# Loading the first token block as two column parts, one on each DMA queue, ahead of everything else, with the matmuls in alternating order

## The chip, the cores and the metric

The kernel runs on one core of a Trainium2 chip. The metric is the time of one execution on the device, in microseconds (us); lower is better. The profile's span, from the first to the last instruction, is about 1.5 us shorter than that time.

## The reference

Two matrix products with a SiLU between them, in bf16, for 2048 tokens of width 640 and a hidden width of 1728:

```python
B, S, D, F = 1, 2048, 640, 1728
def reference(x, w1, w2):
    h = jnp.einsum("bsd,df->bsf", x, w1)
    h = _silu(h)
    out = jnp.einsum("bsf,fd->bsd", h, w2)
    return out
```

## The kernel before

The matmuls of this kernel read tokens with their features on the partitions. For the first chunk of 512 tokens (four blocks of 128) TensorE makes that itself: it multiplies each 128x128 piece of x by an identity matrix (`transpose`), and ScalarE and VectorE copy the result from PSUM to `xT`. The other three chunks come through transposing DMAs later. The first 512 columns of w1 come in five slabs of 128 rows, one for each feature tile d. `early(d, j0, j1)` multiplies slab d with blocks j0 to j1-1, as soon as both are there. Before any data has landed TensorE runs matmuls on constants (`busy`), the warm-ups.

The issue order of the loads, on the two queues (SP and ACT):

```python
        def on_sync(sp):
            # load_x(j): block j, 160 KB.   load_slab(d): slab d, 128 KB
            load_x(0)
            for d in range(0, DT, 2):
                load_slab(d)
            for j in range(2, TPC):
                load_x(j)
            for g, (a, b) in enumerate(((FB, FM), (FM, F))):   # the rest of w1
                sp.dma_start(
                    out=w1_sb[:, :, a:b], in_=w1_v[:, :, a:b]
                ).then_inc(sem_w1g[g], 16)
            sp.wait_ge(sem_w1g[1], 16)
            # ... transposing loads of chunks 1 to 3, then w2 ...

        def on_scalar(act):
            act.dma_start(
                out=x_sb[:, 1, :], in_=xf[P:2 * P, :]
            ).then_inc(sem_xb[1], 16)
            for d in range(1, DT, 2):
                act.dma_start(
                    out=w1_sb[:, d, 0:FB], in_=w1_v[:, d, 0:FB]
                ).then_inc(sem_w1[d], 16)
            # ...
```

TensorE's early phase (W_FIRST = 12, W_SECOND = 15):

```python
            busy(W_FIRST)
            need(sem_id, 2)
            busy(W_SECOND)
            transpose(0)
            transpose(1)
            for j in range(2):
                for d in range(TA):          # TA = 2
                    early(d, j, j + 1)
            early(2, 0, 2)
            early(3, 0, 2)
            transpose(2)
            early(4, 0, 2)
            transpose(3)
            for d in range(3):
                early(d, 2, 3)
            for d in range(3):
                early(d, 3, 4)
            for d in range(3, DT):
                early(d, 2, 4)
            # ... from here on: 512-wide matmuls, 240 + 20 of the first product, 294 of the second
```

## Time and profile before

| | before |
|---|---|
| time, median of the first three executions | 127.17 us (126.99 to 127.23) |
| span of the profiled execution | 125.7 us |
| first transpose starts | 3.76 us |
| clock opens (first start after which 128-wide matmuls follow 56 ns apart instead of 107) | 6.3 us |
| first 512-wide matmul of the main phase starts | 10.47 us |

First, from the page of the kernel before: the span, the busy time of each engine, and the chain of work that ended last.

```profile
span 125.7 us, 1492 instructions
...
PE 123.1 (98%) x661; PEld 60.4 (48%) x661; DVE 12.2 (10%) x20; ACT 37.0 (29%) x65; POOL 0.7 (1%) x6
...
PE 98%; ACT 0%; issue 0%
PE ps L343 47%; PE ps L309 41%; PE ps L254 4%; PE ps L223 2%; PE ps L300 2%; PE ps L239 1%; ACT o_sb L380 0%
```

TensorE (PE) is the chain: nothing else holds up the end. Lines 343, 309 and 300 are the main phase; 223 are the warm-ups, 239 the transposes and 254 the early matmuls. The change touches only the last three, 7.8% of the span (2.4, 1.4 and 4.0%).

Next, the timeline of TensorE up to 11 us. The columns are start, busy us, engine and line, what it is, the count, and in brackets idle time before it with what ended that.

```profile
0.78 3.04 PE L223 MATMUL ps<-const-bfloat16-1.0 128*128 128x128 bf16 x27 [0.78 <-PEq L421]
3.76 1.25 PE L239 MATMUL ps<-ident,x_sb 128*128 128x128 bf16 x10
4.80 2.63 PE L254 MATMUL ps<-xT,w_sb 128*128 128x128 bf16 x24
7.26 0.44 PE L239 MATMUL ps<-ident,x_sb 128*128 128x128 bf16 x5
7.54 0.60 PE L254 MATMUL ps<-xT,w_sb 128*128 128x256 bf16 x4
7.98 0.44 PE L239 MATMUL ps<-ident,x_sb 128*128 128x128 bf16 x5
8.26 2.38 PE L254 MATMUL ps<-xT,w_sb 128*128 128x128 bf16 x32
10.47 0.81 PE L309 MATMUL ps<-xT,w_sb 128*128 128x512 bf16 x3
```

Matmuls overlap (a warm-up is listed with 312 ns and the next starts after 107), so the busy column is no measure of holes. Those show in the single starts of the trace: on the slow clock one 128-wide matmul starts every 107 ns, its slot, and what a step is longer than that is a hole. Below, "cold" is time before the clock opens and "warm" time after it, and a load "lands" when its completion is signalled. Before the first transpose the step is 256 ns, a hole of 0.15 us; there is no other in the early phase.

### The profile page before, as it was taken

What the parts mean: (1) busy time and instruction counts of PE and PEld (TensorE: products, weight loads), DVE (VectorE), ACT (ScalarE), POOL (GpSimd) and SP (SyncE); (2) the same over time, 40 slices, a digit from 0 to 9 for tenths busy, and PEclk for the clock granted to TensorE, in tenths of its full rate; (3) what the DMA queues carried; (4) which work ended last, traced back from release to release, by engine and by line L of the source; (5) the groups of instructions that cost most, each with busy time, mean ns of one, the idle gap of its engine ahead of it and who ended that gap; (6) DMA issues with size and microseconds to landing.
All of it is one profiled execution on the core that took longest, in us unless ns stands there. A gap on an engine that the chain in (4) does not pass through costs nothing.

```text
span 125.7 us, 1492 instructions
## 1 busy us (share of the span) xinstructions
PE 123.1 (98%) x661; PEld 60.4 (48%) x661; DVE 12.2 (10%) x20; ACT 37.0 (29%) x65; POOL 0.7 (1%) x6
## 2 busy tenths in 40 slices
PE   7999999999999999999999999999999999999994
PEld 7996444444444444444444444443444443444452
DVE  0330000000000000000000000000700003920421
ACT  3327655555555555555540000001500000000000
POOL 2000000000000000000000000000000000000000
DMA  3992999992000000000000000000346000631022
GB/s 106 350 374 89 216 201 201 273 387 83 0 0 0 0 3 0 0 0 5 0 0 0 0 0 0 0 5 0 73 94 219 0 0 0 257 113 52 0 104 94
DMA packets 17014, 10.37 MB, mean 82 GB/s; under 512 B 10736, under 2 KB 17008, under 8 KB 17008
## 3 DMA queue, kind: packets, MB, share of 16 engines
q1 hardware_dynamic: 16432, 9.82, 26.8%
q10 hardware_dynamic: 576, 0.46, 1.1%
q8 instruction: 5, 0.08, 0.3%
q14 instruction: 1, 0.01, 0.0%
HBM read 5.16 MB, written 2.62 MB: 62 GB/s over the span
## 4 chain that ended last, share of the span: by engine, by line
PE 98%; ACT 0%; issue 0%
PE ps L343 47%; PE ps L309 41%; PE ps L254 4%; PE ps L223 2%; PE ps L300 2%; PE ps L239 1%; ACT o_sb L380 0%
## 5 line engine op out<-in xcount | busy, mean ns | idle before, releaser
L309 PE MATMUL ps<-xT,w_sb 128*128 128x512 bf16 x240 | 52.0, 379 | 0.0
L343 PE MATMUL ps<-w_sb,hT 128*128 128x512 bf16 (+2 forms) x221 | 45.6, 367 | 0.0
L373 ACT ACTIVATE hT<-ps 128x512 bf16<-128x512 f32 x52 | 30.6, 598 | 23.9 <-PE ps L309 22.2
L309 PEld LDWEIGHTS ps<-xT,w_sb 128*128 128x128 bf16 x240 | 23.5, 98 | 28.1
L343 PEld LDWEIGHTS ps<-w_sb,hT 128*128 128x128 bf16 x221 | 20.8, 98 | 24.6 <-issue 0.6
L399 DVE CAST o_sb<-ps 128x512 bf16<-128x512 f32 (+1 forms) x16 | 10.0, 677 | 104.7 <-PE ps L343 104.7
L343 PE MATMUL ps<-hT,w_sb 128*128 128x512 bf16 x52 | 11.4, 379 | 0.0
L380 ACT CAST o_sb<-ps 128x128 bf16<-128x128 f32 x1 | 0.3, 266 | 34.2 <-PE ps L343 34.2
L380 ACT CAST oT<-ps 128x512 bf16<-128x512 f32 x4 | 2.1, 599 | 22.3 <-PE ps L343 22.3
L343 PEld LDWEIGHTS ps<-hT,w_sb 128*128 128x128 bf16 x52 | 5.0, 98 | 6.3 <-issue 0.4
L254 PE MATMUL ps<-xT,w_sb 128*128 128x128 bf16 (+1 forms) x60 | 5.6, 258 | 0.0
L254 PEld LDWEIGHTS ps<-xT,w_sb 128*128 128x128 bf16 x60 | 4.8, 111 | 0.2
L223 PE MATMUL ps<-const-bfloat16-1.0 128*128 128x128 bf16 x27 | 3.0, 312 | 0.8 <-PEq L421 0.8
L223 PEld LDWEIGHTS ps<-const-bfloat16-1.0 128*128 128x128 bf16 x27 | 2.8, 148 | 0.7 <-issue 0.7
L392 DVE CAST xT<-ps 128x384 bf16<-128x384 f32 x4 | 2.2, 558 | 6.8 <-PE ps L239 6.8
L366 ACT CAST xT<-ps 128x256 bf16<-128x256 f32 x4 | 1.5, 372 | 3.5 <-PE ps L239 3.5
L300 PE MATMUL ps<-xT,w_sb 128*64 128x512 bf16 x20 | 2.3, 381 | 0.0
L343 PE MATMUL ps<-w_sb,hTl 64*128 64x512 bf16 (+2 forms) x17 | 2.2, 366 | 0.0
L239 PE MATMUL ps<-ident,x_sb 128*128 128x128 bf16 x20 | 2.1, 265 | 0.0
L361 ACT ACT_TABLE_LOAD x1 | 1.3, 1283 | 2.1 <-issue 2.1
L239 PEld LDWEIGHTS ps<-ident,x_sb 128*128 128x128 bf16 x20 | 1.7, 120 | 0.2 <-DMA x_sb<-in_x_dram 0.2
L300 PEld LDWEIGHTS ps<-xT,w_sb 128*64 128x64 bf16 x20 | 1.0, 110 | 1.2 <-ACT hT L373 0.4
(11 smaller groups left out, 3.7 us busy)
## 6 DMA issues: line engine op xcount, KB each, us to landing
out_dram<-o_sb SPq DMA_DIRECT2D x15, 160.0 KB, 1.8
w_sb<-in_w_dram SPq DMA_DIRECT2D x1, 1120.0 KB, 7.6
w_sb<-in_w_dram SPq DMA_DIRECT2D x1, 960.0 KB, 5.6
w_sb<-in_w_dram SPq DMA_DIRECT2D x1, 880.0 KB, 7.2
w_sb<-in_w_dram SPq DMA_DIRECT2D x1, 640.0 KB, 5.2
x_sb<-in_x_dram SPq DMA_DIRECT2D x3, 160.0 KB, 4.0
w_sb<-in_w_dram SPq DMA_DIRECT2D x3, 128.0 KB, 3.4
w_sb<-in_w_dram ACTq DMA_DIRECT2D x2, 128.0 KB, 3.8
```

The source lines that it names most:

```text
L223: pe.matmul(ps[:, KF - 1, 0:P], lhsT=ones[:, 0:P], rhs=ones[:, 0:P], start=True, stop=True,)
L239: ins = pe.matmul(ps[:, ba + (d >= TA), k * P:(k + 1) * P], lhsT=x_sb[:, j, d * P:(d + 1) * P], rhs=ident[:, :], start=True, stop=True,)
L254: ins = pe.matmul(ps[:, f, j0 * P:j1 * P], lhsT=w1_sb[:, d, f * P:(f + 1) * P], rhs=xT[:, d, j0 * P:j1 * P], start=(d == 0 and j0 == 0), s ...
L300: ins = pe.matmul(ps[h * FL:(h + 1) * FL, b, :], lhsT=w1_sb[:, d, NF * P:F], rhs=xT[:, d, (c + h) * CH:(c + h + 1) * CH], start=(d == 0), ...
L309: ins = pe.matmul(ps[:, b, :], lhsT=w1_sb[:, d, f * P:(f + 1) * P], rhs=xT[:, d, c * CH:(c + 1) * CH], start=(d == 0), stop=(d == DT - 1),)
L343: ins = pe.matmul(ps[:, bank, 0:width], lhsT=w_op if kind == "T" else h_op, rhs=h_op if kind == "T" else w_op, start=(first2[key] == i), s ...
L361: act.activation(out=warm_sb[:, :], in_=nc.const_aps.tensor(0.0, [P, 1], fp32), func=ACT.Silu)
L366: act.copy(out=xT[:, 0:TA, j * P:(j + 1) * P], in_=ps[:, 4 + 2 * (j % 2), 0:TA * P].rearrange("p (d s) -> p d s", s=P),).then_inc(sem_cpa, 1)
L373: act.activation(out=dst, in_=ps[:, i % NB, :], func=ACT.Silu).then_inc(sem_act1, 1)
L380: act.copy(out=dst, in_=ps[:, place[key], 0:dst.shape[-1]]).then_inc(sem_evb, 1)
L392: dve.tensor_copy(out=xT[:, TA:DT, j * P:(j + 1) * P], in_=ps[:, 5 + 2 * (j % 2), 0:(DT - TA) * P].rearrange("p (d s) -> p d s", s=P),).th ...
L399: dve.tensor_copy(out=o_sb[:, key[1], cols], in_=ps[:, place[key], cols]).then_inc(sem_eva, 1)
```

## The change

The intent is to start real work sooner. Block 0 goes ahead of everything, 3 of its 5 column tiles on one queue and 2 on the other, so that only 160 KB travel before it is complete, and three warm-ups fewer stand in its way. Block 1 moves to the second place on the scalar queue. The third queue entry on SP is now block 2 rather than slab 2, and the matmul order alternates accordingly: each further block is transposed and used before the next slab is needed. The rest of w1 comes in three pieces instead of two.

```diff
-    W_FIRST, W_SECOND = 12, 15
+    W_FIRST, W_SECOND = 12, 12
 ...
-            load_x(0)
-            for d in range(0, DT, 2):
+            sp.dma_start(
+                out=x_sb[:, 0, 0:DS], in_=xf[0:P, 0:DS]
+            ).then_inc(sem_xb[0], 16)
+            load_slab(0)
+            load_x(2)
+            load_slab(2)
+            load_x(3)
+            for d in range(3, DT):
                 load_slab(d)
-            for j in range(2, TPC):
-                load_x(j)
-            for g, (a, b) in enumerate(((FB, FM), (FM, F))):
+            for g, (a, b) in enumerate(G_COLS):          # three pieces
 ...
+                    if j == 0 and d >= TS:               # in transpose(j)
+                        need(sem_xr, 16)
 ...
+            transpose(2)
             early(2, 0, 2)
-            early(3, 0, 2)
-            transpose(2)
-            early(4, 0, 2)
-            transpose(3)
             for d in range(3):
                 early(d, 2, 3)
-            for d in range(3):
+            transpose(3)
+            early(3, 0, 3)
+            for d in range(4):
                 early(d, 3, 4)
-            for d in range(3, DT):
-                early(d, 2, 4)
+            early(4, 0, 4)
 ...
             act.dma_start(
+                out=x_sb[:, 0, DS:D], in_=xf[0:P, DS:D]
+            ).then_inc(sem_xr, 16)
+            act.dma_start(
                 out=x_sb[:, 1, :], in_=xf[P:2 * P, :]
             ).then_inc(sem_xb[1], 16)
-            for d in range(1, DT, 2):
-                act.dma_start(
-                    out=w1_sb[:, d, 0:FB], in_=w1_v[:, d, 0:FB]
-                ).then_inc(sem_w1[d], 16)
+            act.dma_start(
+                out=w1_sb[:, 1, 0:FB], in_=w1_v[:, 1, 0:FB]
+            ).then_inc(sem_w1[1], 16)
```

## The prediction

> **What bounds the kernel.** TensorE. The page has it busy 98% of the 125.7 us span, and the chain of waits is TensorE from 0.78 to 123.87 us, with 0.1% "issue". Matmul starts in the trace: 27 warm-up matmuls on constants from 0.78 us, a 256 ns step (107 is regular, so 0.15 us of wait) until token block 0 has landed at 3.71 us, then no hole up to the first 512-wide matmul at 10.47 us. Up to 6.28 us the 128-wide starts are 107 ns apart, afterwards 56 ns (256-wide 109, 512-wide 216). The page "TensorE: Matmul & The Clock Gate" (Part 1) of the Trainium skill calls this the clock gate, opened by a free-running activity window of about 3.4 us; the trace agrees on the two rates and on the opening, about 5.5 us after the first matmul.
>
> The time is wait-free TensorE work, of which what runs before 6.28 us runs at half rate. Early data is worth something only where TensorE has no work, and a cold slot gained is worth a warm one (56 ns), as the clock's opening doesn't move.
>
> **What the change does.**
> - Warm-ups 27 -> 24: their slots end at 3.29 us instead of 3.61.
> - Block 0 lands earlier, as 160 KB travel first instead of 320 KB. At the 360 to 390 GB/s of the DMA view 160 KB are about 0.4 us, less the slow ramp (92 GB/s from 1.7 to 2.2 us): I estimate 3.40 us. Its transposes then start at 3.45 instead of 3.76, behind the same small hole: 0.31 us cold.
> - Block 1 is now second on its queue. Before, it landed at 3.90, slabs 0 and 1 at 4.31 and 4.49 (320 and 576 KB in all). Interpolating at 448 KB I estimate 4.2 us. Block 0's five transposes end at about 3.98, so a new hole of about 0.2 us opens. Block 1's transposes start at about 4.22 instead of 4.26: most of the gain is taken back; 0.04 us cold, 0.02 at the end, remain.
> - Slab 1, now third on the scalar queue, is estimated at 4.85 us with a straggler to 5.6 (slab 3, third there before, came at 6.02). Needed at about 5.2: perhaps 0 to 0.4 us of wait.
> - Matmul order: the early phase keeps its 10,240 columns but takes 56 matmuls instead of 60, at about 2.5 ns fixed each: 0.01 us. Later loads arrive in time.
> - Weights' rest in three pieces: first need at 10.4 us against a landing by about 8.7; the last still about 11.2. The transposing load behind it landed at 17.0 and is needed at 20.2: 3 us of slack.
>
> **Sum.** -0.02 -0.01, plus 0 to 0.2 for slab 1, less up to 0.15 if block 1 comes as early as block 0's transposes end: about -0.05. I predict **127.12 us**, range 126.8 to 127.4. Faster by over 2%: 0.005; within 2%: 0.985; slower: 0.01.
>
> **What would show it.** 24 warm-ups; first transpose at about 3.45 us; a hole of about 0.2 us ahead of transpose 6; still 107 ns until near 6.3 us; first 512-wide matmul at about 10.4; the 113.3 us from it to the end unchanged.
>
> **What would make it wrong.** The clock opening at another time: each us earlier or later is worth 0.5 us. A block late while warm, which costs in full. Holes that keep the activity window from counting as busy. Smaller rows ramping more slowly.

## The result, and the profile after

| | before | after |
|---|---|---|
| time, median of 6 executions | 127.0 us (126.81 to 127.23) | 127.23 us (126.77 to 129.16) |
| ratio of the fast executions, 95% interval | | 1.0011 (0.9989 to 1.0033) |
| profiled execution: time, span | 127.22, 125.7 us | 126.77, 125.3 us |
| first transpose | 3.76 us | 3.29 us |
| clock opens | 6.3 us | 5.4 us |
| first 512-wide matmul of the main phase | 10.47 us | 10.05 us |
| from there to the end of the span | 115.24 us | 115.25 us |

A ratio is the mean time of one kernel's fast executions over that of the other's in the same rounds, so it is not quite the ratio of the medians. The execution of 129.16 us is slow and is not in it. The prediction's "113.3 us" from the main phase to the end is taken from the chain, to TensorE's end (10.63 to 123.90 us there); the table goes on to the end of the span. Both stayed as they were.

The page of the kernel after (line 353 is 343 of before, 319 is 309, 265 is 254, 250 is 239, 310 is 300):

```profile
span 125.3 us, 1470 instructions
...
PE 121.6 (97%) x643; PEld 59.0 (47%) x654; DVE 12.2 (10%) x20; ACT 37.1 (30%) x65; POOL 0.7 (1%) x6
...
PE 94%; DMA 2%; issue 1%; ACTq 0%; ACT 0%
PE ps L353 47%; PE ps L319 41%; PE ps L265 4%; DMA x_sb<-in_x_dram 2%; PE ps L310 2%; PE ps L250 1%; ACTq L364 0%; ACT o_sb L392 0%
```

A DMA of x is now in the chain, and the warm-ups (line 232) are not. The 643 matmuls are not all there were: 11 records are missing from this trace, as the 654 weight loads show, and most of the 1% "issue" stands at such gaps. The timeline of TensorE up to 11 us:

```profile
0.78 2.72 PE L232 MATMUL ps<-const-bfloat16-1.0 128*128 128x128 bf16 x24 [0.78 <-PEq L433]
3.29 0.74 PE L250 MATMUL ps<-ident,x_sb 128*128 128x128 bf16 x5
4.23 0.71 PE L250 MATMUL ps<-ident,x_sb 128*128 128x128 bf16 x5 [0.20 <-DMA x_sb<-in_x_dram]
4.74 1.37 PE L265 MATMUL ps<-xT,w_sb 128*128 128x128 bf16 x16
5.95 0.44 PE L250 MATMUL ps<-ident,x_sb 128*128 128x128 bf16 x5
6.23 1.30 PE L265 MATMUL ps<-xT,w_sb 128*128 128x256 bf16 x16
7.37 0.44 PE L250 MATMUL ps<-ident,x_sb 128*128 128x128 bf16 x5
7.65 2.57 PE L265 MATMUL ps<-xT,w_sb 128*128 128x384 bf16 x23
10.05 1.24 PE L319 MATMUL ps<-xT,w_sb 128*128 128x512 bf16 x5
```

And the head of its chain in order of time (start, us, what):

```profile
0.74 0.40 ACTq L364
1.14 0.03 issue
1.17 3.02 DMA x_sb<-in_x_dram
4.19 0.05 issue
4.23 0.71 PE ps L250 x5
```

Block 0's transposes start 0.47 us sooner and finish their slots at 3.83 us. Then TensorE waits 0.41 us for block 1 (the step between starts is 516 ns against a regular 107), whose load was issued at 1.17 us and lands at 4.19. Block 1's transposes start at 4.23 us, against 4.26 before: of the 0.47 us, 0.03 are left. A second, smaller hole of 0.08 us stands ahead of slab 1's matmuls at 5.25 us. The landings, each the last of the sixteen completions in the trace, say why:

| landed at, us | block 0 | block 1 | slab 0 | slab 1 | block 2 | slab 2 | slab 3 | slab 4 |
|---|---|---|---|---|---|---|---|---|
| before | 3.71 | 3.90 | 4.31 | 4.49 | 6.58 | 5.05 | 6.02 | 6.25 |
| after | 2.99 and 3.16 | 4.19 | 3.95 | 5.20 | 5.00 | 5.40 | 6.51 | 6.84 |

Block 0, slab 0 and block 2, which moved up or have less ahead of them, landed earlier (block 3 too: 6.20 us for 7.02); block 1 and slabs 1 to 4, which have more ahead of them, landed later. The Trainium skill, page "DMA: Bandwidth & Descriptors", section "Issuing engines are not separate DMA queues", says that DMAs of different engines run on the same 16 DMA engines and interleave, whoever issued them; these landings are in keeping with it. They don't prove it for block 1: it is also issued 0.43 us later than before (1.17 us for 0.74), being second on its queue, and lands 0.29 us later. No run here separates the later issue from the sharing.

Still the profiled execution is 0.4 us shorter. That is the clock. On the slow clock a 128-wide matmul takes 107 ns, afterwards 56; in this execution the change came at 5.4 us, in that of before at 6.3. An opening that is 0.9 us sooner is worth half of that, 0.45 us. So the start of the main phase less half the opening time is a fair measure of the early phase (an estimate, good only where TensorE has no holes after the opening): before 10.47 - 6.3/2 = 7.3, after 10.05 - 5.4/2 = 7.4 us. At equal opening the change gains nothing, and the main phase takes 115.24 us in either kernel.

### The profile page after: what moved, and what is told of

Same layout as the page of the kernel before. It is cut to its first block, busy times and chain, and to the rows that moved or that the text cites. A ratio compares the mean times of both kernels' runs of the same rounds, so it can differ in the third digit from the quotient of the medians.

```text
span 125.3 us, 1470 instructions
## 1 busy us (share of the span) xinstructions
PE 121.6 (97%) x643; PEld 59.0 (47%) x654; DVE 12.2 (10%) x20; ACT 37.1 (30%) x65; POOL 0.7 (1%) x6
## 2 busy tenths in 40 slices
DMA packets 17814, 10.37 MB, mean 83 GB/s; under 512 B 10768, under 2 KB 17808, under 8 KB 17808
## 4 chain that ended last, share of the span: by engine, by line
PE 94%; DMA 2%; issue 1%; ACTq 0%; ACT 0%
PE ps L353 47%; PE ps L319 41%; PE ps L265 4%; DMA x_sb<-in_x_dram 2%; PE ps L310 2%; PE ps L250 1%; ACTq L364 0%; ACT o_sb L392 0%
## 5 line engine op out<-in xcount | busy, mean ns | idle before, releaser
L319 PEld LDWEIGHTS ps<-xT,w_sb 128*128 128x128 bf16 x240 | 23.5, 98 | 28.3
L265 PE MATMUL ps<-xT,w_sb 128*128 128x128 bf16 (+3 forms) x55 | 5.2, 247 | 0.1
L265 PEld LDWEIGHTS ps<-xT,w_sb 128*128 128x128 bf16 x56 | 3.8, 102 | 0.8
```

The lines of the kernel that those rows point to most:

```text
L265: ins = pe.matmul(ps[:, f, j0 * P:j1 * P], lhsT=w1_sb[:, d, f * P:(f + 1) * P], rhs=xT[:, d, j0 * P:j1 * P], start=(d == 0 and j0 == 0), s ...
L319: ins = pe.matmul(ps[:, b, :], lhsT=w1_sb[:, d, f * P:(f + 1) * P], rhs=xT[:, d, c * CH:(c + 1) * CH], start=(d == 0), stop=(d == DT - 1),)
```

## The experiments

Each ran together with the kernel before, in the same session on the same chip; the sessions used three chips (8, 0 and 1), so only ratios to the kernel before compare from one run to another. Theory A is that of the prediction: the start that block 0 gained is taken back by a wait for the next load, and executions differ by when the clock opens. Theory B is that the 0.4 us of the profile are a real gain of the change, lost elsewhere in other executions. Theory C came up with the execution of 129.16 us: a hole too long keeps a window of activity from counting, so the clock opens one window later. The Trainium skill, page "TensorE: Matmul & The Clock Gate", Part 1, gives the window as 3413 ns and free-running; at half rate a window lost should cost 1.7 us (an estimate from that page's figure). The ranges of the opening in the expectations, 4.2 to 7.6 us with warm-ups, are estimates from it too: one to two windows after the first matmul at 0.78 us. The profiles with warm-ups and no hole over 0.7 us opened at 4.3 to 6.6 us.

### The changed kernel again

No edit.

> The changed kernel once more, unaltered. Theory A (the early start is eaten by the new wait for block 1, and the 0.4 us that the profile shows are the clock opening earlier in that one execution): the loads land as before (block 0 at about 3.1 us, block 1 at about 4.2), the hole ahead of block 1's transposes is again 0.3 to 0.5 us, but the step from 107 to 56 ns comes at another time, anywhere between 4.2 and 7.6 us, and the start of the first 512-wide matmul moves by half of that. Ratio 0.998 to 1.003. Theory B (the 0.4 us are a real gain of the change, lost again somewhere after the early phase in the timed runs): the first 512-wide matmul again at about 10.05, whatever the clock did, and the lost time visible later in the trace. Theory C (the new hole keeps the activity window from counting as busy in some executions, which opens the clock a whole window, 3.4 us, later and costs 1.7 us: the execution of 129.16 us): about one execution in six again near 129 us.

Measured: ratio 1.002 (0.9999 to 1.0042); all executions from 126.88 to 127.51 us, none near 129. In the profiled one, block 0 landed at 3.00 and 3.17 us, block 1 at 4.32, the hole ahead of block 1 was 0.55 us, the clock opened at 6.2 us and the main phase began at 10.51: 10.51 - 6.2/2 = 7.4 us again. Theory B is out: with a later opening the "gain" of 0.4 us is gone, while the early phase runs as before. Theory C's one in six was not seen; six executions are too few to rule it out.

### Constant matmuls in the hole

```diff
             transpose(0)
+            busy(4)
             transpose(1)
```

> The change, with four more constant matmuls (4 x 107 = 0.43 us) put between block 0's and block 1's transposes, where TensorE had a hole of 0.41 us. Theory A: the hole is dead time and takes them for nothing: block 1's transposes start at about 4.25 us as before, ratio to the kernel before 0.998 to 1.003, no difference from the changed kernel beyond 0.1%. Theory C: with the hole filled no execution is near 129 us, and the mean falls below that of the changed kernel. If warm-ups cost time in themselves, 0.2 to 0.4 us slower than the changed kernel.

Measured: 126.65 to 127.40 us, ratio 1.0003 (0.9978 to 1.0028). The four matmuls cost nothing that shows; the mean is 0.17% below the changed kernel's in the same rounds (126.87 against 127.09 us), more than the 0.1% expected but within what the intervals leave open. No execution was near 129 us, but the changed kernel had none in these rounds either, so this run says nothing on theory C. The opening came very early here, at 4.4 us, and the timeline shows what that is worth:

```profile
3.82 0.58 PE L232 MATMUL ps<-const-bfloat16-1.0 128*128 128x128 bf16 x4
4.35 0.45 PE L250 MATMUL ps<-ident,x_sb 128*128 128x128 bf16 x5
4.64 0.39 PE L265 MATMUL ps<-xT,w_sb 128*128 128x128 bf16 x4
5.38 0.84 PE L265 MATMUL ps<-xT,w_sb 128*128 128x128 bf16 x12 [0.35 <-DMA w_sb<-in_w_dram]
```

On the fast clock TensorE is through with block 0 and slab 0 at 4.86 us and then stands idle for 0.51 us until slab 1 lands at 5.33. The main phase began at 10.16 us although the clock opened 1 us before that of the changed kernel's first profile. An early opening gives nothing where the data aren't there.

### Block 1's wait taken away (wrong result)

```diff
-                need(sem_xb[j], 16)
+                src = 0 if j == 1 else j
+                need(sem_xb[src], 16)
 ...
-                        lhsT=x_sb[:, j, d * P:(d + 1) * P],
+                        lhsT=x_sb[:, src, d * P:(d + 1) * P],
```

> Wrong on purpose: block 1's transposes read block 0's data, which is there, so that nothing waits for block 1's landing (its load is still made). Theory A: they follow block 0's at once, at about 3.83 instead of 4.23 us, but the gain does not reach the end: the first matmuls on slab 1 then wait for its landing at about 5.2 us, in a hole of about 0.4 us there, so the ratio stays within 0.2% of the changed kernel's. If block 1 alone bounds the early phase: no other hole, and 0.41 us of cold time gained, 0.2 us at the end at equal clock opening.

Measured: ratio 1.0014 (0.9988 to 1.004). No gain shows, but the 0.2 us (0.16%) of the other expectation would not stand out of this interval; the trace has to decide. The profiled execution is one of 145.23 us with a granted clock of 0.856, a slow one; its later times are not used. Up to 5.2 us its matmuls start 107 ns apart as in the fast ones, and the order of events there is the point: block 1's transposes follow block 0's without a hole, and the hole of 0.41 us stands ahead of slab 1's first matmul, at 5.19 us. Waits of TensorE from 3 to 10.5 us in that execution (engine, waited for: us in total, times, longest):

```profile
PEld ps L266 <- DMA w_sb<-in_w_dram: 0.5, 1, 0.5
PE ps L266 <- DMA w_sb<-in_w_dram: 0.2, 1, 0.2
```

The wait moved from block 1 to slab 1, at the same length, as theory A expected.

### Slab 1's wait taken away too (wrong result)

```diff
 # with the edit above, and in early(d, j0, j1):
-                need(sem_w1[d], 16)
+                need(sem_w1[d if j0 >= 2 or d > 1 else 0], 16)
 ...
-                        lhsT=w1_sb[:, d, f * P:(f + 1) * P],
+                        lhsT=w1_sb[:, d if j0 >= 2 or d > 1 else 0, f * P:(f + 1) * P],
```

> Wrong on purpose, a step further than the run without the wait for block 1, whose hole only moved to the first matmul on slab 1 (4.76 to 5.19 us): now the early matmuls on slab 1 for blocks 0 and 1 use slab 0's weights, which are there. Theory A: ten transposes and sixteen matmuls without a hole from 3.29 us; 0.45 to 0.55 us of cold time gained on the changed kernel, so at equal clock opening the first 512-wide matmul 0.2 to 0.27 us earlier; ratio to the changed kernel about 0.998, still hard to see among executions that differ by up to 0.8 us through the opening. If something else bounds the early phase, a third hole of about 0.4 us ahead of slab 2 or block 2.

Measured: ratio to the kernel before 1.0003 (0.9981 to 1.0026). In the profile there is no hole between 3.29 us and the main phase; its chain runs through the warm-ups without a DMA:

```profile
0.77 2.72 PE ps L232 x24
3.49 1.07 PE ps L251 x10
4.56 1.71 PE ps L266 x16
6.27 0.47 PE ps L251 x5
6.74 1.11 PE ps L266 x16
```

The clock opened at 6.6 us and the main phase began at 10.37: 10.37 - 6.6/2 = 7.1 us, against 7.4 for the changed kernel in its two profiles. So the two waits together cost about 0.3 us, a little over the expected 0.2 to 0.27. In the times that doesn't stand out of the spread of the openings. Against the kernel before (7.3) 0.2 us remain: that is what the change could have been worth if its loads had come for nothing.

### Block 1 in parts as well

```diff
             ).then_inc(sem_xb[0], 16)
+            sp.dma_start(
+                out=x_sb[:, 1, 0:DS], in_=xf[P:2 * P, 0:DS]
+            ).then_inc(sem_xb[1], 16)
             load_slab(0)
 ...
-                out=x_sb[:, 1, :], in_=xf[P:2 * P, :]
-            ).then_inc(sem_xb[1], 16)
+                out=x_sb[:, 1, DS:D], in_=xf[P:2 * P, DS:D]
+            ).then_inc(sem_xr1, 16)
 # ... and transpose(1) waits for both parts
```

> Blocks 0 and 1 both loaded as two column parts, one on each queue, ahead of the slabs; nothing else altered. Theory A: block 1 lands at about 3.6 to 3.8 us instead of 4.19, slab 0 at about 4.2, slab 1 at about 4.5 to 4.7 instead of 5.2, all before they are needed (3.83, 4.36 and 4.79): no holes, 0.4 to 0.5 us of cold time gained on the changed kernel, 0.2 to 0.27 us at the end at equal clock opening, ratio about 0.998. If more DMAs on a queue only push back what comes behind them, slab 1 is as late as in the changed kernel and the hole stands ahead of its matmuls.

Measured: ratio 1.0069 (1.0023 to 1.0115), slower than before, and in two kinds: 127.19, 127.35, 127.38 and 128.89, 129.10, 129.24 us. (The record classes the last two as slow and leaves them out of the ratio; the granted clock reads 1.000 in all six.) The expectation failed. Block 1 did land at 3.40 and 3.59 us, but slab 0 only at 5.70 and slab 1 at 5.90, 1.2 to 1.5 us later than expected. The profile is of the slower kind (128.89 us). Two lines of TensorE's timeline, and the same stretch by windows (busy us of each engine, granted clock, DMA share, GB/s):

```profile
3.29 1.27 PE L254 MATMUL ps<-ident,x_sb 128*128 128x128 bf16 x10
5.74 1.89 PE L269 MATMUL ps<-xT,w_sb 128*128 128x128 bf16 x16 [1.18 <-DMA w_sb<-in_w_dram]
```

```profile
3.30:4.40 1.10, 1.10 (x12) 0.99 (x10) 0.34 (x1) 0.83 (x4) 0.00 (x0) 1.00 0.87 211
4.40:5.70 1.30, 0.16 (x2) 0.00 (x0) 0.75 (x2) 0.25 (x1) 0.00 (x0) 1.00 0.96 301
```

From 3.3 to 4.4 us the DMA engines were busy for 87% of the time and moved only 211 GB/s; why the packets were slower there stays open. By the single starts TensorE issued nothing from 4.35 to 5.74 us, and the clock opened only at 8.8 us, later than in any other profile. If a window of 3413 ns ended there, the one before ended at 5.4, and TensorE had been idle for 1.0 us of it. The means of the two kinds are 1.8 us apart, close to half a window. This gave theory C its second case.

### The same, with that hole filled

```diff
 # on top of "block 1 in parts as well"
             transpose(1)
+            busy(13)
```

> The kernel with blocks 0 and 1 both in parts, which had executions of two kinds (127.2 to 127.4 and 128.9 to 129.2 us); in its profiled one, of the slower kind, TensorE stood idle for 1.4 us ahead of slab 0's matmuls and the clock opened only at 8.74 us. Added: 13 constant matmuls (13 x 107 = 1.39 us) in that place. Theory C (a window of 3.41 us with too long a hole does not count, and the next one opens the clock, 1.7 us dearer): the slower kind is gone, the clock opens before 7.6 us in the profile, and all executions lie between 126.8 and 127.7 us although work was added. Rival (the slower kind is slower transfers, and the clock opens late with them by chance): the two kinds stay, the slower one at 129 us or more.

Measured: 127.16 to 127.81 us, ratio 1.0052 (1.0031 to 1.0072). The slower kind is gone, although 13 matmuls were added. Slab 0 still landed late, at 5.52 us, so the transfers had not become faster; the clock opened at 6.2. The expected upper end of 127.7 was missed by 0.1. The chain:

```profile
3.49 1.07 PE ps L254 x10
4.56 1.39 PE ps L236 x13
5.95 1.05 PE ps L269 x16
```

That is what theory C says: the same late data, without the idle time, and no execution that looks as if it had lost a window. The counts alone, 3 of 6 and then 0 of 6, come about by chance once in eleven times, and the two runs were on different chips (8 and 0); the profiles, with slab 0 as late and the clock open 2.6 us sooner, are one execution each. Nor is the filling free: the faster kind of the kernel without it is at about 1.004 of the kernel before (from the means), this one at 1.005.

### No warm-ups

```diff
-    W_FIRST, W_SECOND = 12, 12
+    W_FIRST, W_SECOND = 0, 0
```

> The changed kernel without any warm-up matmul. Theory A: block 0's transposes start at about 3.2 us, hardly earlier than with them, as data sets that, so the 24 warm-ups cost nothing; but the clock now opens between 6.6 and 10 us instead of 4.2 to 7.6, on average 2.5 us later, so the time is 1.0 to 1.7 us longer: ratio 1.008 to 1.014. If the warm-ups are mere filler: ratio 1.000 to 1.002.

Measured: 127.88 to 128.94 us, ratio 1.0131 (1.0101 to 1.0161), inside the range. The first transpose started at 3.13 us, only 0.17 us before that of the changed kernel; the clock opened at 7.6 us. So the warm-ups take next to no time from the data, and set against the changed kernel's ratios (1.0011 and 1.002) they are worth 1.1 to 1.2%, nearly all of it through the clock: in the profiles it opened 2.2 us later than in the changed kernel's first, half of which is 1.1, and the main phase began 1.2 us later. The rest can be the data: block 1 landed at 4.59 us here, for 4.19.

### The new loads with the old matmul order

The order of `early` and `transpose` is that of the kernel before; loads and warm-ups are those of the change.

```diff
-            transpose(2)
             early(2, 0, 2)
+            early(3, 0, 2)
+            transpose(2)
+            early(4, 0, 2)
+            transpose(3)
             for d in range(3):
                 early(d, 2, 3)
 ...
```

> The changed kernel's loads and warm-ups with the matmul order of the kernel before (block 2's transposes after slabs 2 and 3 of blocks 0 and 1). Theory A: the order alone is worth little: the matmuls of slab 3 now come at about 6.4 us against a landing at about 6.5, a hole of 0 to 0.3 us in warm time, so 0 to 0.3 us slower than the changed kernel at equal clock opening: ratio to the kernel before 1.000 to 1.004. If the alternating order carries a gain of its own that the new loads only pay for: 0.5 us or more slower than the changed kernel.

Measured: ratio 1.0064 (1.002 to 1.0109), again in two kinds: 127.00, 127.31, 127.35 and 128.77, 129.14, 129.25 us. That is above the expected 1.004, but the ratio contains the execution of 128.77 us (the two slower ones are left out); the faster three alone are at about 1.003 (from the means), inside the expectation. What was not expected is the slower kind. The profile is of the faster kind, with the clock open from 4.7 us. By the single starts it has holes of 0.67 us ahead of block 1, 0.17 ahead of slab 1 and 0.60 ahead of slab 3; the last on TensorE's timeline:

```profile
6.94 0.61 PE L265 MATMUL ps<-xT,w_sb 128*128 128x256 bf16 x4 [0.43 <-DMA w_sb<-in_w_dram]
```

The changed kernel has block 2's transposes and twelve matmuls on it in that place. The order, then, does not save time against before, but with the new loads the old one leaves TensorE waiting there.

### The same, with its holes filled

```diff
 # on top of "the new loads with the old matmul order"; the constant matmuls
 # write to a part of PSUM that nothing else uses
             transpose(0)
+            busy(6)
             transpose(1)
 ...
+            busy(8)
             early(3, 0, 2)
```

> The changed kernel's loads with the old matmul order had three of six executions at 128.8 to 129.3 us, and in a profiled fast one holes of 0.67, 0.17 and 0.60 us ahead of block 1, slab 1 and slab 3. Added: 6 constant matmuls ahead of block 1's transposes and 8 ahead of the first matmuls on slab 3. Theory C: TensorE is never idle long enough to lose a window, so all executions lie within 126.8 to 127.8 us and none above 128, with more work than the kernel that had them. Rival (the slower executions are slower transfers): still two kinds, some at 128.7 us or more.

Measured: 127.09 to 127.95 us, ratio 1.006 (1.0036 to 1.0084); one execution lies 0.15 us over the expected range, none above 128. The slower kind is gone here too. Taken together, the two kernels with long holes had 6 of 12 executions above 128.7 us (6 of 13 with the second look below), and with the holes filled 0 of 12, which chance alone gives about once in a hundred times or less. This pair was on different chips as well (0 and 1), but on chip 0, in one session, the kernel with block 1 in parts and its hole filled had no slow execution while the old order had three. Two holes were filled at once here, so which of them costs the window isn't shown, and the filled kernel at 1.006 is slower than the faster kind without filling (1.003).

### A second look at it

No edit to "the new loads with the old matmul order".

> A second look at the kernel with the new loads and the old matmul order, in the hope of a profile of its slower kind. If it takes about 127.3 us: clock opening between 4.2 and 7.6 us. If it takes 128.8 us or more, theory C: the opening comes after 7.6 us, and the window of 3.41 us before the one that opened holds more than 0.5 us of idle TensorE; the time from the first 512-wide matmul of the second token chunk's units to the end is the same as in all other executions. Rival: the opening is early and the loss is a transfer that lands 1.5 us late, or is later in the trace.

Measured: one execution, 126.95 us, of the faster kind, with the clock open from 4.4 us and holes of 0.53, 0.39 and 0.21 us in the same three places. It doesn't answer the question: what the clock does in this kernel's slower kind (opening late, or closing again after the warm holes) was not seen.

### Block 0 whole again

```diff
-                out=x_sb[:, 0, 0:DS], in_=xf[0:P, 0:DS]
+                out=x_sb[:, 0, :], in_=xf[0:P, :]
             ).then_inc(sem_xb[0], 16)
 ...
-            act.dma_start(
-                out=x_sb[:, 0, DS:D], in_=xf[0:P, DS:D]
-            ).then_inc(sem_xr, 16)
```

> The changed kernel with its named part undone: block 0 comes whole on the first queue, block 1 first on the other, as before the change; 24 warm-ups, three weight pieces and the alternating order stay. Theory A: block 0 lands at about 3.7 us again, block 1 at about 3.9; a cold hole of 0.4 to 0.5 us ahead of block 0's transposes, then none; at equal clock opening the first 512-wide matmul within 0.1 us of the changed kernel's and of before's; ratio 0.998 to 1.002. If the split of block 0 carries a gain, this is 0.2 us or more slower than the changed kernel. Theory C: the hole is one and short, so no execution near 129 us.

Measured: 126.09 to 127.17 us, ratio 0.9977 (0.9952 to 1.0002), at first sight the best of all. Its chain starts with block 0's load:

```profile
0.73 2.95 DMA x_sb<-in_x_dram
3.68 0.05 issue
3.73 1.22 PE ps L248 x10
4.94 0.89 PE ps L263 x16
5.84 0.28 PE ps L248 x5
```

There is one cold hole, of 0.44 us, ahead of the first transpose at 3.73 us, and none to speak of after it (0.03 us). The clock opened at 4.8 us and the main phase began at 9.78: 9.78 - 4.8/2 = 7.4 us, as with the split. So at equal opening the split, the named part of the change, brought nothing.

### Block 0 whole, and that hole filled

```diff
 # on top of "block 0 whole again"
-    W_FIRST, W_SECOND = 12, 12
+    W_FIRST, W_SECOND = 12, 16
```

> The run with block 0 whole again (0.9977 of the kernel before, interval up to 1.0002) had a cold hole of 0.44 us ahead of block 0's transposes, as it kept 24 warm-ups. Here 28, which fill it: only the alternating order, the load order of the slabs and the three weight pieces are left of the change. Theory A: block 0's transposes start at about 3.75 us, no hole after that in the early phase, at any clock opening; the gain over the kernel before is that an early opening (4.2 to 6 us) finds its data: ratio 0.996 to 0.999, and no execution above 127.4. If the first measurement was luck of the openings: 1.000 within 0.15%.

Measured: 126.66 to 127.17 us, ratio 1.0002 (0.9978 to 1.0025). The expected gain did not come. Block 0 landed at 3.78 us, which left a cold hole of 0.11 us. The clock opened at 4.3 us, and TensorE then met warm holes of 0.18 us ahead of the first early matmul (it waits for copies to `xT` and for slab 0) and 0.21 us ahead of slab 2, contrary to the expectation of none. So the 0.9977 got no support; the kernel that gave it was not run a second time. No version was found that beats the kernel before by more than the noise.

### Profiles side by side

Clock opening, start of the main phase, and the span from there to the end, read from the single starts:

| kernel | opens, us | main phase starts, us | span from there, us | note |
|---|---|---|---|---|
| before | 6.3 | 10.47 | 115.24 | no hole but 0.15 us |
| after | 5.4 | 10.05 | 115.25 | cold holes 0.41, 0.08 |
| after, again | 6.2 | 10.51 | 115.25 | cold hole 0.55 |
| both waits away | 6.6 | 10.37 | 115.24 | no hole |
| block 0 whole | 4.8 | 9.78 | 115.23 | cold hole 0.44 |
| hole filled | 4.4 | 10.16 | 115.24 | holes 0.11 ahead of block 1, 0.51 warm |
| block 0 whole, filled | 4.3 | 9.96 | 115.23 | holes 0.11 cold, 0.18 and 0.21 warm |
| no warm-ups | 7.6 | 11.25 | 115.24 | cold hole 1.0 |
| block 1 in parts | 8.8 | 12.15 | 115.24 | cold hole 1.39 |
| the same, filled | 6.2 | 10.93 | 115.23 | 13 matmuls more |
| old order | 4.7 | 10.60 (by its neighbour; the record is missing) | 115.24 | holes 0.67 cold, 0.17 and 0.60 warm |
| old order, second look | 4.4 | 10.24 | 115.24 | holes 0.53, 0.39, 0.21 |
| the same, filled | 4.5 | 10.38 | 115.24 | 14 matmuls more |

The run with block 1's wait taken away is left out, as its execution was slow. The main phase is the same in all the others to 0.02 us: all differences lie in the first 12 us.

## Why the prediction was right, point by point

The time (127.12 us predicted, 127.23 measured, ratio 1.0011) and its reason, a gain taken back by the next load, were right. That the time came within 0.1 us is in part luck: the five executions besides the slow one spread over 0.7 us, and the forecast gain of 0.05 us is less than the runs can resolve. What the runs confirm is the mechanism.

- "Its transposes then start at 3.45 instead of 3.76": the landing of block 0, estimated at 3.40 us, was mis-sized. It landed at 2.99 and 3.16, so the warm-ups set the start, at 3.29, and there was no "small hole".
- "Block 1's transposes start at about 4.22 instead of 4.26": 4.23 measured, with block 1 landed at 4.19 for an estimated 4.2. The hole was 0.41 us instead of 0.2, as block 0 was done sooner by the same amount. Interpolating the landing from the bytes that travel ahead of a load worked for this one. Taking the wait away showed that it bounds nothing by itself: the hole moved to slab 1.
- "Slab 1 ... is estimated at 4.85 us with a straggler to 5.6": 5.20, and a hole of 0.08 us, inside the range.
- "Matmul order: ... 0.01 us. Later loads arrive in time." This step was incomplete. In the changed kernel they do arrive in time, but that rests on the new order: with the old one the two profiles had warm holes of 0.60 and 0.21 us ahead of slab 3, and three of the first six executions took 1.8 us more. The count of matmuls was the smallest part of what the order does.
- "the trace agrees ... on the opening", of the window of 3.4 us, says only that the 5.5 us from the first matmul lie between one window and two.
- "still 107 ns until near 6.3 us" and "first 512-wide matmul at about 10.4": 5.4 and 10.05 in the first profile, 6.2 and 10.51 in the second. This was named as what would move the time by 0.5 us for each us of opening, and it did.
- "Holes that keep the activity window from counting as busy" was named as a risk. The runs support it for the kernel with block 1 in parts (opening at 8.8 us, slower kind gone when filled). Whether the changed kernel's one execution of 129.16 us, out of 12, was such a case is only argued: it was not profiled.
- "the last still about 11.2": the last weight piece landed at 12.33 us, a miss of 1.1 us. The three pieces cost nothing all the same: the transposing load of the second chunk landed at 17.7 us instead of 17.0, still 2 us before its use at 19.8.

What stays open: exactly how much idle time a window may hold; what the clock does in the slower kind with the old order; and why slab 0 and 1 came more than 1 us later than expected when four part loads ran ahead of them.

## What to carry to other kernels

Here, moving one load to the front moved the others back, so before splitting a load find the next load that the engine will wait for; if that one is about as late, the gain ends there. While TensorE is on its slow clock, a slot gained (107 ns) is worth half at the end (56 ns), and the opening of the clock moves single executions by more than such a change: compare profiles at equal opening. A wait in the warm-up phase can be filled with constant matmuls: filling took the slow executions of 129 us away in both kernels that had them often, but it did not make their faster executions any faster (1.005 and 1.006 of the kernel before with the filling, 1.004 and 1.003 without). It repairs the bad case; it is no gain.

## What the Trainium skill lacked or had wrong

- "TensorE: Matmul & The Clock Gate" (Part 1) doesn't say how much idle time a window may hold and still count as busy. The runs bracket it, if the window is the page's 3413 ns: in the changed kernel a hole of 0.55 us before the opening at 6.2 us still counted, and with the old order one of 0.67 us before the opening at 4.7; about 1.0 us of idle time in the window up to 5.4 us (block 1 in parts, one profile) did not, and the clock opened at 8.8.
- The same page, "Back-to-back issue gap", gives a sustained spacing with weight loads of about 81 ns for 128 columns and 131 ns for 512. Here, with one weight load for every matmul, the starts are 56 ns and 216 ns apart on the open clock, which agrees with the page's figures for isolated matmuls.
- The same page's Part 4 gives about 275 ns for a 128x128 transpose inside a kernel in TensorE's transpose mode, and says that the full clock doesn't engage for that mode. It gives no figure for a transpose made as an ordinary matmul by an identity matrix, as here. In the trace of the kernel before, one lasts 219 to 314 ns (ends are modelled), and the starts are 56 ns apart on the open clock, 107 before.
- No page gives a way to work out when a load lands once another is put ahead of it. Here it could be interpolated from the bytes ahead in one case (block 1: 4.19 us for an estimated 4.2), and not in another (slab 0 behind four part loads: 5.70 us for an expected 4.2).
